# Blockwise causal attention and RWKV channel mix in one kernel: the opening of batch 0 is cut finer and every queue gets a new order

## The chip, the cores and the metric

The kernel runs on one core of one Trainium2 chip, as a single launch. The metric is device time in microseconds (us) of one execution, the median of the runs shown. Inputs are float32 arrays in device memory, the output is a float32 array of 8 x 576 x 512 there; products run in 16-bit types and accumulate in float32.

## The reference

Attention over 8 batches, 8 heads, 576 positions and 64 columns per head, with a mask by blocks of 64 positions; then a channel mix with a token shift over the joined heads. Cut to what matters:

```python
scores = np.matmul(q, k.transpose(0, 1, 3, 2)) / np.sqrt(64)
mask = (pos[:, None] // 64) >= (pos[None, :] // 64)
attn = softmax(np.where(mask, scores, -1e9))          # + 1e-9 in the denominator
x = (attn @ v)                                        # then (B, S, H * D): 8 x 576 x 512
x_prev = x shifted by one position, zero in front
xk = mu_k * x + (1 - mu_k) * x_prev
xr = mu_r * x + (1 - mu_r) * x_prev
kk = np.maximum(xk @ w_k, 0.0)                        # 512 -> 1024
out = sigmoid(xr @ w_r) * ((kk * kk) @ w_v)           # 1024 -> 512
```

## The kernel before

**Attention, batch by batch.** For each batch q and k come in as four tiles of 128 x 1152 float32 (two groups g of four heads, n = 0 for q and 1 for k). Each tile goes through the same steps: a load (tile `t_ld`, queue SP, L272), a cast to bfloat16 (`t_nl`, L251 on ACT or L255 on DVE and POOL), nine transposing products on PE into one PSUM tile (`t_s`, L367; the task is called `turn b g n`), and a copy out of PSUM into `t_qkt` (task `ev b g n`, L251 or L255). In batches 5 to 7 a transposing DMA (L353) does the last two steps instead. v comes as two tiles that are cast to `t_vo`.

Scores are computed transposed (keys on the partitions), in twelve tasks `sc b part i`: `part` 0 or 1 picks which head of a pair, i = 0 to 5 which key blocks (L426). Each is followed by one exponential on ACT (`ex b part i`, L435) into a float16 tile `t_e`. No maximum is taken off first. Then come the column sums of the exponentials, 60 small products with a one-hot matrix `pick` (task `av b 0 S`, L477), and the products with v (`av b 0 A` and `av b 0 B`, L486). DVE transposes the sums (`t1`, L514), takes reciprocals (`rec`, L519), small copies put them in their places (`fix`, L251 or L255), two transposes with broadcast spread them (`t2`, L545), and two multiplications each (`norm`, L555 and L559) write the attention's result to `t_xt`.

**Channel mix, chunk by chunk.** `d` (L581) forms x minus its shifted self, `mul` (L597) forms x + (mu - 1) d into XK and XR, in float16; XK and XR are rings of 1536 rows, so that a chunk of 512 rows crosses batch bounds. There are nine chunks c. For each: `pk c jc` (L644, eight tasks of four products 128x512), a relu (L622 on ACT, L624 on DVE), a square (L630 on ACT, L632 on DVE and POOL) into `t_k`; `pr c jt` (L666, four tasks) with a tanh (L675); `pv c jt` (L694, four tasks of eight products), the gated result on DVE (`o`, L702) and a store (L709). The weights are loaded early, through the same `t_ld` tiles, and cast to WK, WR and WV by tasks `w` (L251, L252, L255, L256).

**What sets the order.** Every step above is a task with a number, its dependences and its buffers. The string ORDER lists the 946 task numbers in the order in which they are issued; each engine and the SP queue carries out its share strictly in that order and waits where an operand or a buffer is missing. The string PLACE picks the engine of every task that more than one engine could do. Buffers are rings: six `t_ld`, four `t_nl`, sixteen `t_e`, three PSUM tiles `t_s` of two banks for turns, scores, sums and products with v, two PSUM tiles `t_mm` of one bank for the channel mix. A load waits in the SP queue until the cast that empties its `t_ld` tile is done, and so holds up what is behind it.

**Unread products.** A word such as `9+14` in ORDER puts 14 extra products 128x512 of the identity with itself ahead of task 9 (L264, function `unread`); they write to a free `t_mm` tile, and nobody reads them. They depend on nothing that comes from device memory, so they run while PE would wait. There are 49 of them, all before the channel mix starts: 14 ahead of the first turn, 9 ahead of the second, 26 ahead of later turns and scores of batches 0 to 2.

In batch 0 every score waits for all four copies `ev 0 g n`, each of 1152 columns:

```python
        deps = [evac[b, g, n] for g in range(2) for n in range(2)]
```

The sums of a batch are one task that waits for all twelve exponentials (`fnS`, L492; `sums`, L460).

## Time and profile before

| | |
|---|---|
| median of 3 runs | 258.75 us (258.72 to 259.55) |
| the profiled execution | 259.53 us; its span is 257.7 us |
| PE busy | 246.6 us, 96% of the span |
| DVE, ACT, POOL busy | 192.4, 181.5, 89.7 us |
| the 49 unread products | 15.7 us of PE's busy time |
| read from and written to device memory | 33.56 and 9.44 MB |

The profile is of one execution; its times are counted from the start of the span. PE is TensorE's matmuls, PEld its weight loads, DVE is VectorE, ACT ScalarE, POOL GpSimd, SP the queue that issues all DMA transfers. A row of the time line gives the start, the duration, the engine, the line, the operation, output and input, the count of merged instructions, and in brackets the engine's idle time just before with what ended it. Idle time of an engine costs only where another waits for it.

### The profile page before, as it was taken

How to read it: one execution, taken by the hardware profiler on the slowest of the kernel's cores; microseconds unless marked ns; L12 is line 12 of the kernel's file. 1: busy time of each engine (PE TensorE's matmuls, PEld its weight loads, DVE VectorE, ACT ScalarE, POOL GpSimd, SP SyncE). 2: the span in 40 equal slices, each digit the busy share in tenths (PEclk: the TensorE clock that was granted, in tenths of full speed). 3: DMA queues.
4: the chain of work that ended last, by engine and by line, in shares of the span. 5: the costliest groups of instructions: out<-in, count | busy, mean ns of one | idle time of the engine just before them, and what ended most of it. 6: DMA issues, size and time to landing. Idle time of an engine off the chain costs nothing.

```text
span 257.7 us, 6524 instructions
## 1 busy us (share of the span) xinstructions
PE 246.6 (96%) x2718; PEld 123.0 (48%) x2718; DVE 192.4 (75%) x274; ACT 181.5 (70%) x251; POOL 89.7 (35%) x74
## 2 busy tenths in 40 slices
PE   7989789999999999999999999999999999999994
PEld 2546454544555445554454454445444544444452
DVE  1814799899779989878799896985997597763412
ACT  1299698987889698676889888687689480550630
POOL 1024384680038313470273103130712543260220
PEclk9999999999999999999999999999999999999999
DMA  7999979979699399996990899999907300303014
GB/s 256 399 265 260 347 237 241 323 217 282 196 274 235 86 188 200 267 198 129 264 149 4 196 174 263 239 154 217 227 6 186 112 4 0 122 0 122 4 61 184
DMA packets 93150, 46.96 MB, mean 182 GB/s; under 512 B 80696, under 2 KB 80960, under 8 KB 93120
## 3 DMA queue, kind: packets, MB, share of 16 engines
q1 hardware_dynamic: 93120, 46.54, 75.4%
q8 instruction: 21, 0.34, 0.6%
q14 instruction: 9, 0.07, 0.1%
HBM read 33.56 MB, written 9.44 MB: 167 GB/s over the span
## 4 chain that ended last, share of the span: by engine, by line
PE 80%; DVE 8%; ACT 6%; POOL 2%; issue 2%; DVEq 0%; POOLq 0%; ACTq 0%
PE t_mm L644 24%; PE t_mm L694 23%; PE t_mm L666 10%; PE t_s L426 8%; PE t_s L486 6%; ACT t_e L435 5%; PE t_s L477 4%; PE t_s L367 3%; PE t_mm L264 3%; DVE t_xt L559 2%; POOL t_k L632 1%; DVE t_rt L545 1%; POOL t_d L581 1%; DVE WV L256 1%; ACT t_qkt L251 1%
## 5 line engine op out<-in xcount | busy, mean ns | idle before, releaser
L435 ACT ACTIVATE t_e<-t_s 128x1024 f16<-128x1024 f32 (+1 forms) x96 | 88.2, 979 | 16.8 <-PE t_s L426 15.0
L644 PE MATMUL t_mm<-XK,WK 128*128 128x512 f16 x288 | 68.5, 379 | 0.3
L694 PE MATMUL t_mm<-WV,t_k 128*128 128x512 f16 (+1 forms) x296 | 66.1, 374 | 0.9 <-DVE WV L256 0.5
L632 POOL TENSOR_TENSOR t_k<-t_kr 128x512 f16<-128x512 f32 x31 | 36.4, 1184 | 59.7 <-ACT t_kr L622 42.6
L622 ACT ACTIVATE t_kr<-t_mm 128x512 f32<-128x512 f32 x55 | 32.6, 598 | 27.8 <-PE t_mm L644 27.5
L694 PEld LDWEIGHTS <-t_k 128*128 128x128 f16 x296 | 27.6, 98 | 34.5 <-issue 3.0
L644 PEld LDWEIGHTS <-WK 128*128 128x128 f16 x288 | 26.5, 97 | 32.9 <-issue 4.9
L702 DVE SCALAR_TENSOR_TENSOR t_o<-t_t,t_mm 128x512 f32<-128x512 f32 (+1 forms) x37 | 24.7, 671 | 22.3 <-PE t_mm L694 13.2
L426 PE MATMUL t_s<-t_qkt 64*64 64x512 bf16 (+7 forms) x640 | 31.0, 290 | 4.1 <-ACT t_qkt L251 2.0
L666 PE MATMUL t_mm<-WR,XR 128*128 128x512 f16 x144 | 34.8, 379 | 0.0
L255 POOL CAST t_vo<-t_ld 128x1152 f16<-128x1152 f32 x12 | 14.3, 1189 | 48.6 <-DVE XR L597 16.1
L597 DVE SCALAR_TENSOR_TENSOR XK<-t_d,MU,t_xt 128x576 f16<-128x576 f32 (+2 forms) x40 | 29.4, 758 | 0.8 <-POOL t_d L581 0.7
L597 DVE SCALAR_TENSOR_TENSOR XR<-t_d,MU,t_xt 128x576 f16<-128x576 f32 (+2 forms) x40 | 28.1, 727 | 0.1
L255 POOL CAST t_nl<-t_ld 128x1152 bf16<-128x1152 f32 x12 | 14.8, 1244 | 32.3 <-DMA t_ld<-in_k_dram 15.7
L675 ACT ACTIVATE t_t<-t_mm 128x512 f32<-128x512 f32 x36 | 21.1, 595 | 6.6 <-PE t_mm L666 6.5
L426 PEld LDWEIGHTS <-t_qkt 64*64 64x64 bf16 x640 | 15.0, 105 | 21.9 <-issue 18.8
L545 DVE STREAM_TRANSPOSE t_rt<-t_rc 128x1152 f32<-128x1152 f32 x16 | 22.0, 1377 | 1.5 <-ACT t_rc L251 1.1
L486 PE MATMUL t_s<-t_e,t_vo 64*64 64x64 f16 (+7 forms) x640 | 22.8, 284 | 0.1
L581 POOL TENSOR_TENSOR t_d<-t_xt 128x1152 f32<-128x1152 f32 x8 | 17.4, 2172 | 10.5 <-DVE t_xt L559 6.8
L666 PEld LDWEIGHTS <-XR 128*128 128x128 f16 x144 | 13.3, 97 | 16.1 <-issue 1.3
L486 PEld LDWEIGHTS <-t_vo 64*64 64x64 f16 x640 | 15.9, 107 | 8.4 <-issue 1.9
L251 ACT COPY t_qkt<-t_s 128x1152 bf16<-128x1152 bf16 x12 | 13.2, 1121 | 9.1 <-PE t_s L367 9.1
(40 smaller groups left out, 205.4 us busy)
## 6 DMA issues: line engine op xcount, KB each, us to landing
t_ld<-in_v_dram SPq DMA_DIRECT2D x32, 288.0 KB, 5.9
out_dram<-t_o SPq DMA_DIRECT2D x35, 256.0 KB, 2.6
t_ld<-in_k_dram SPq DMA_DIRECT2D x10, 576.0 KB, 6.5
t_ld<-in_q_dram SPq DMA_DIRECT2D x10, 576.0 KB, 5.4
t_ld<-in_q_dram SPq DMA_DIRECT2D x12, 288.0 KB, 5.1
t_ld<-in_k_dram SPq DMA_DIRECT2D x12, 288.0 KB, 5.7
t_ld<-in_moe_w_k_dram SPq DMA_DIRECT2D x4, 512.0 KB, 6.7
t_ld<-in_moe_w_v_dram SPq DMA_DIRECT2D x4, 512.0 KB, 5.7
```

The source lines that it names most:

```text
L255: return e.tensor_copy(dst, src)
L426: nc.tensor.matmul(PS[g * D:g * D + D, x, col:col + n], qkt[rows, ka:ka + D], qkt[rows, qa:qa + n], start=True, stop=True)
L435: nc.scalar.activation(new(ebuf[key])[:, :, 0:width], new(m)[:, :, 0:width], AF.Exp, scale=ISQ)
L486: nc.tensor.matmul(dst(slice(y * D, (y + 1) * D), u, x, q0, n), new(vo_buf[b])[u * D:u * D + D, 2 * x + y, t], new(ebuf[key])[u * D:u * D ...
L545: nc.vector.transpose(new(rt[x])[:, 0:2 * W].rearrange("p (n r) -> p n r", r=QC), new(rc)[:, x].rearrange("p u n -> p (u n)").unsqueeze(2) ...
L597: return nc.vector.scalar_tensor_tensor((XK, XR)[kr][:, cc, g:g + w], new(d)[:, u * n + at - lo:u * n + at - lo + w], MU1[:, kr, cc:cc + 1 ...
L622: nc.scalar.activation(new(kr), new(m), AF.Relu)
L632: return e.tensor_tensor(dst(), KR, KR, ALU.mult)
L644: nc.tensor.matmul(ps, WK[:, cc, jc * P:(jc + 1) * P], XK[:, cc, at:at + CH], start=(cc == 0), stop=(cc == CCn - 1))
L666: nc.tensor.matmul(ps, XR[:, cc, g % R:g % R + P], WR[:, cc], start=(cc == 0), stop=(cc == CCn - 1))
L694: nc.tensor.matmul(ps[:, 0:w], k2[:, jc, jt * P:(jt + 1) * P], WV[:, jc, cols], start=(jc == 0), stop=(jc == JCn - 1))
L702: nc.vector.scalar_tensor_tensor(new(o)[:, 0:w], new(tb)[:, cols], 1.0, new(m)[:, 0:w], ALU.add, ALU.mult)
```

## The change

Four things are edited, and the rest of the program is as it was.

1. The copies out of the turns of batch 0 are cut in two along the transposed columns: half y (0 or 1) holds the keys and queries of `part` y. Each copy `ev 0 g n` of 1152 columns becomes `ev 0 g n 0` and `ev 0 g n 1` of 576, each with an engine of its own. A score of part y waits only for the four halves y.
2. The sums of batch 0 are two tasks on the same PSUM tile: `av 0 0 P` with the 40 products that need only the exponentials i = 0 to 3, and `av 0 0 S` with the remaining 20, which goes on in the same accumulation.
3. ORDER has new numbers throughout (951 tasks), with 36 unread products instead of 49: 9 ahead of the first turn instead of 14, then none, 3 and 3 ahead of the other turns of batch 0 where 9, none and 1 stood.
4. PLACE is new. All four copies of batch 1's turns are on DVE (two were on ACT); batch 0's first cast and all four of batch 1's are on POOL.

The core of the diff (ORDER and PLACE cut to a line):

```diff
-7 8 9+14 10 11 12 13+9 15 16 17 18 3 4 5+1 6 96 14 49+4 50 61 57 58 62
+13 14 15+9 0 1 18 19 20 21 22 3 4 8 9 5+3 6 7 101 102 93 94 17 10+3 11
...
+        parts = 2 if b == 0 else 1
+        for y in range(parts):
+            def ev(eng, me, y=y):
+                pst = new(m)[:, :, :].rearrange("p a b -> p (a b)").bitcast(BF)
+                w, h = 2 * S // parts, P // parts
+                convert(eng, new(qkt_buf[b])[
+                    :, at + y * w:at + y * w + w].rearrange(
+                        "q (p j) -> q p j", j=JT),
+                    pst[:, 0:2 * S].rearrange("q (j p) -> q p j", p=P)[
+                        :, y * h:y * h + h])
...
-        deps = [evac[b, g, n] for g in range(2) for n in range(2)]
+        deps = [evac[b, g, n, part if b == 0 else 0]
+                for g in range(2) for n in range(2)]
...
+        FIRST = 4 if b == 0 else 0
...
+                if (key[2] < FIRST) != early:
+                    continue
...
+            opens = 4 if early or not FIRST else 0
+            ends = len(runs) if early else len(runs) - 4
             for n_, (c, a, z, j, t, src, _) in enumerate(runs):
                 nc.tensor.matmul(
                     PA[c * QC:(c + 1) * QC, a:z], pick[:, j], src,
-                    start=n_ < 4, stop=n_ >= len(runs) - 4)
+                    start=n_ < opens, stop=n_ >= ends)
...
+            exps = exps + [add(
+                f"av {b} {part} P", "PE", lambda eng, me: fnS(eng, me, True),
+                [ready[key] for key in some],
+                [m["S"]] + [ebuf[key] for key in some])]
```

**Place one: DVE, from its first cast on.** `t_nl` are casts of loaded tiles (`t_ld`), `t_qkt` copies out of PSUM, `t_tt` the transposed sums. Before:

```order
L255 CAST t_nl_67<-t_ld_58 128x2x9x64
L255 COPY t_qkt_74<-t_s_152 128x1152
L255 CAST t_nl_68<-t_ld_59 128x2x9x64
L255 CAST t_nl_69<-t_ld_60 128x2x9x64
L255 CAST t_nl_70<-t_ld_61 128x2x9x64
L255 COPY t_qkt_74<-t_s_153 128x1152
L255 CAST t_nl_67<-t_ld_63 128x2x9x64
```

After:

```order
L255 CAST t_nl_68<-t_ld_59 128x2x9x64
L255 CAST t_nl_69<-t_ld_60 128x2x9x64
L255 CAST t_nl_70<-t_ld_61 128x2x9x64
L255 COPY t_qkt_74<-t_s_154 128x576
L255 COPY t_qkt_74<-t_s_152 128x576
L255 COPY t_qkt_74<-t_s_153 128x576
```

The first tile's cast has gone to POOL, and no copy stands between the casts of batch 0 any more. Behind these rows DVE now has one more half copy, the four copies of batch 1 (`t_qkt_75`), one cast of batch 2 and then the sums; before, it had two of batch 1's copies and two more casts ahead of the sums.

**Place two: ACT, from the last exponentials of batch 0 on.** `t_e` are exponentials, `t_qkt` copies out of the turns, `t_rc` the small copies of the reciprocals. Before:

```order
L435 ACTIVATE t_e_94<-t_s_154 128x2x320
L435 ACTIVATE t_e_95<-t_s_153 128x2x320
L251 COPY t_qkt_75<-t_s_154 128x1152
L251 COPY t_qkt_75<-t_s_152 128x1152
L251 COPY t_rc_112<-t_rc_112 32x36 x4
L251 COPY t_qkt_74<-t_s_154 128x1152
L435 ACTIVATE t_e_96<-t_s_154 128x1024
```

After:

```order
L441 ACTIVATE t_e_94<-t_s_152 128x1024
L441 ACTIVATE t_e_95<-t_s_153 128x1024
L441 ACTIVATE t_e_96<-t_s_154 128x1024
L251 COPY t_rc_112<-t_rc_112 32x36 x2
L441 ACTIVATE t_e_97<-t_s_153 128x1024
L441 ACTIVATE t_e_98<-t_s_153 128x1024
```

The three copies of turns between batch 0's exponentials and batch 1's are gone from there; `t_e_96`, batch 1's first exponential, stands ahead of the reciprocals' copies.

**Place three: DVE, from the last weight cast on.** WV is the cast of w_v, `t_d` the difference, XK and XR the mixes, `t_o` the gated results of chunk 0. Before:

```order
L256 TENSOR_SCALAR WV<-t_ld_58 128x1024
L597 SCALAR_TENSOR_TENSOR XK<-t_d_121,MU_176,t_xt_104 128x576
L581 TENSOR_TENSOR t_d_122<-t_xt_104 128x1152
L597 SCALAR_TENSOR_TENSOR XR<-t_d_122,MU_176,t_xt_104 128x576
L597 SCALAR_TENSOR_TENSOR XK<-t_d_122,MU_176,t_xt_104 128x576
L702 SCALAR_TENSOR_TENSOR t_o_145<-t_t_138,t_mm_159 128x512
L702 SCALAR_TENSOR_TENSOR t_o_146<-t_t_141,t_mm_158 128x512
```

After:

```order
L256 TENSOR_SCALAR WV<-t_ld_59 128x1024
L601 TENSOR_TENSOR t_d_121<-t_xt_104 128x1152
L617 SCALAR_TENSOR_TENSOR XR<-t_d_121,MU_176,t_xt_104 128x576
L617 SCALAR_TENSOR_TENSOR XK<-t_d_121,MU_176,t_xt_104 128x576
L722 SCALAR_TENSOR_TENSOR t_o_145<-t_t_138,t_mm_159 128x512
L617 SCALAR_TENSOR_TENSOR XR<-t_d_122,MU_176,t_xt_104 128x576
L617 SCALAR_TENSOR_TENSOR XK<-t_d_122,MU_176,t_xt_104 128x576
```

Three XR mixes now stand ahead of or between the four XK mixes of batch 1, where one stood; DVE has one `d`, seven mixes and three gated results to do from here to the last XK mix, five mixes, one `d` and three gated results before.

28 lines of the change are left out of this document (13 added, 15 removed), and 102 rows, old and new, of the table ORDER.

## The prediction, on record before the run

> **What bounds the kernel now.** I read the page's busy times first, then the table by stretches, then the time line of the first 60 us.
>
> ```profile
> PE 246.6 (96%) x2718; PEld 123.0 (48%) x2718; DVE 192.4 (75%) x274; ACT 181.5 (70%) x251; POOL 89.7 (35%) x74
> DMA  7999979979699399996990899999907300303014
> ...
> 0.00:40.00 40.00, 33.25 (x435) 19.02 (x436) 22.96 (x33) 27.30 (x33) 13.67 (x15) 1.00 0.99 291
> 40.00:60.00 20.00, 19.36 (x265) 9.59 (x264) 19.04 (x27) 18.35 (x27) 12.34 (x10) 1.00 0.90 261
> 60.00:240.00 180.00, 179.54 (x1949) 87.20 (x1946) 144.43 (x206) 130.01 (x185) 60.35 (x46) 1.00 0.75 158
> 240.00:258.00 18.00, 14.47 (x75) 7.15 (x73) 6.00 (x10) 5.80 (x10) 3.33 (x3) 1.00 0.24 89
> ...
> L264 PE MATMUL t_mm<-identb 128*128 128x512 bf16 x49 | 15.7, 441 | 1.4 <-POOL identb masks.py:199 1.4
> ```
>
> In the second to fifth rows the columns are the stretch, PE, PEld, DVE, ACT, POOL busy, clock, DMA share, GB/s. From 60 to 240 us PE is busy 179.54 of 180: there is nothing to win, only something to lose. The waste is in the first 40 us: 6.75 us idle and 15.7 us of unread products, which PE fills its waits with. All other PE work is the same after the change, so the time moves with one quantity: how soon the head lets PE run without waits. I take the start of the first `pv` as the mark.
>
> ```profile
> 1.36 5.59 PE L264 MATMUL t_mm<-identb 128*128 128x512 bf16 x14 [1.36 <-POOL identb masks.py:199]
> 4.28 0.76 DVE L255 CAST t_nl<-t_ld 128x1152 bf16<-128x1152 f32 x1 [2.39 <-DMA t_ld<-in_k_dram]
> 6.79 0.67 PE L367 MATMUL t_s<-identb,t_nl 128*128 128x128 bf16 x9
> 7.29 2.11 PE L264 MATMUL t_mm<-identb 128*128 128x512 bf16 x9
> 7.49 1.36 DVE L255 COPY t_qkt<-t_s 128x1152 bf16<-128x1152 bf16 x1 [2.45 <-PE t_s L367]
> 8.77 2.09 DVE L255 CAST t_nl<-t_ld 128x1152 bf16<-128x1152 f32 x3
> 10.96 2.14 ACT L251 COPY t_qkt<-t_s 128x1152 bf16<-128x1152 bf16 x2 [8.94 <-PE t_s L367]
> 13.61 10.46 ACT L435 ACTIVATE t_e<-t_s 128x1024 f16<-128x1024 f32 x12 [0.51 <-PE t_s L426]
> 24.22 2.14 ACT L251 COPY t_qkt<-t_s 128x1152 bf16<-128x1152 bf16 x2 [0.15 <-PE t_s L367]
> 26.44 0.48 DVE L514 STREAM_TRANSPOSE t_tt<-t_s 128x288 f32<-128x288 f32 x1 [3.42 <-ACT t_qkt L251]
> ...
> 27.59 0.91 ACT L251 COPY t_rc<-t_rc 32x36 f32<-32x36 f32 x4 [1.23 <-DVE MU L296]
> ...
> 30.16 1.02 ACT L435 ACTIVATE t_e<-t_s 128x1024 f16<-128x1024 f32 x1 [0.51 <-PE t_s L426]
> ...
> 31.69 1.02 ACT L435 ACTIVATE t_e<-t_s 128x1024 f16<-128x1024 f32 x1 [0.51 <-PE t_s L486]
> ...
> 39.71 2.18 PE L644 MATMUL t_mm<-XK,WK 128*128 128x512 f16 x8
> ...
> 56.67 2.39 DVE L256 TENSOR_SCALAR WV<-t_ld 128x1024 f16<-128x1024 f32 x2
> ...
> 59.20 3.61 PE L694 MATMUL t_mm<-WV,t_k 128*128 128x512 f16 x16 [0.50 <-DVE WV L256]
> ```
>
> The reader sees a chain: the first tile is cast at 5.04, but its turn starts only at 6.79, because fourteen products stand ahead; DVE then holds three casts behind a copy; ACT starts its exponentials at 13.61 and has none left over; the sums reach DVE at 26.44, when ACT's copies are done; from there DVE works almost without a gap until the last WV cast ends at 59.06, and `pv` starts 0.14 later.
>
> **The change, step by step.**
>
> *First turn.* Fourteen products take 5.59 before the turn, 0.40 each, the first ones slower; at 0.43 nine end at 1.36 + 9 x 0.43 = 5.2. The first tile's cast is now POOL's:
>
> ```profile
> 13.79 1.14 POOL L255 CAST t_nl<-t_ld 128x1152 bf16<-128x1152 f32 x1 [12.49 <-DMA t_ld<-in_k_dram]
> ...
> t_ld<-in_k_dram SPq DMA_DIRECT2D x1, 576.0 KB, 3.5
> ...
> t_ld<-in_k_dram SPq DMA_DIRECT2D x1, 576.0 KB, 8.6
> ```
>
> (The last two rows are the first load, issued at 0.73, and the seventh, issued at 5.07: size and time to landing.) The first lands at 4.2, POOL ends at 5.4, the turn starts at 5.5 instead of 6.79. The two small loads of mu are now second in SP's queue; the tiles behind them are spaced by the transfers, not by their issue: (13.7 - 4.2)/6 = 1.58 us from tile to tile. I cost them at nothing, at most 0.8 (two issues).
>
> *Fourth tile and first exponential.* The fourth tile lands at 4.2 + 3 x 1.58 = 9.0; DVE has no copy ahead of it now (before, its cast ended at 10.86, behind the copy at 7.49 and two casts). Cast to 9.8, turn to 10.5. A half copy costs between half a whole one and a whole one, 0.56 to 1.12 on ACT and 0.68 to 1.36 on DVE; a 36-column copy takes 0.91/4 = 0.23, mostly fixed, so I take 0.66 and 0.75. ACT's last half for part 1 ends at 11.2, DVE's second half at 11.3; the score takes 0.4, the first exponential starts near 11.9, 1.7 sooner. But the second score task in PE's order is of part 0 and waits for DVE's fourth half (12.8); the second exponential, a score behind it on PE, starts at about 13.6, so ACT loses 0.7: 1.0 is left.
>
> *Batch 0's exponentials.* Twelve take 10.46: at best 11.9 + 0.7 + 10.46 = 23.1. Batch 1's four copies, now all DVE's, and its turns lie between them on PE. The turn of tile 1 1 1 stands ahead of the last three scores; it is the ninth load, 4.2 + 8 x 1.58 = 16.8, cast on POOL at 18.0. With a PSUM tile `t_s` passed on to each whole copy of 1.36 us, I walk the queues to 23.9 (before: 24.07). Ends: 23.1 and 24.6.
>
> *Sums.* 40 of 60 products run while the last exponential does; 20 remain:
>
> ```profile
> 46.65 1.43 PE L477 MATMUL t_s<-t_e,pick 128*32 128x288 f16 x60
> ```
>
> 1.43/3 = 0.5. `P` stands behind batch 1's first score on PE, which needs batch 1's last copy (22.2 by the same walk), so that it holds nothing up. t1 starts at 24.7 (ends 24.3 and 25.4) instead of 26.44: **-1.7 us**. Before, ACT's two copies at 24.22 stood between; they are now DVE's, hidden under exponentials.
>
> *DVE from t1 to the last WV cast.* Before: 59.06 - 26.44 = 32.6, nearly all busy. After, the list lacks one cast, one whole copy, one relu, one v cast and four small copies, and has one WK cast, two squares and one WV cast more:
>
> ```profile
> 44.97 1.27 DVE L624 TENSOR_SCALAR t_kr<-t_mm 128x512 f32<-128x512 f32 x2
> 46.17 0.74 DVE L255 CAST t_vo<-t_ld 128x1152 f16<-128x1152 f32 x1
> 49.37 0.78 DVE L255 COPY t_rc<-t_rc 32x36 f32<-32x36 f32 x4
> ...
> L632 DVE TENSOR_TENSOR t_k<-t_kr 128x512 f16<-128x512 f32 x17 | 12.7, 776 | 4.2 <-ACT t_kr L622 4.1
> ```
>
> Less: 0.76 + 1.36 + 0.64 + 0.74 + 0.78 = 4.3. More: 0.75 (the other casts) + 2 x 0.78 + 1.2 = 3.5. **-0.8 us.** New waits: the reciprocals' copies stand behind batch 1's exponentials on ACT (up to 1.0 each, two places). The second sums wait for batch 1's last exponential. Where sums and products with v hold two PSUM tiles, batch 1's exponentials share the third and come 31.69 - 30.16 = 1.53 apart; after, five do so from 26.3 to 33.5, three more follow at 0.9 apiece (36.2), then three whole copies at 1.13 (39.6), three exponentials and a relu (43): sums near 43.2 instead of 46.65, just ahead of the second t1 in DVE's list. Together **+0.5**, ends 0 and 2.
>
> *PE.* One score task fewer lies ahead of the first `pv`: **+0.2**. PE itself does not bind: from the first `pk` (39.71 before; about 37.5 after, 2.2 sooner with the XK mixes) it has at most 17.2 us of work to the first `pv` (the 19.5 of before less some waits). If DVE were faster than I think, PE's bound would be near 54.7, a gain of 4.5: the low end.
>
> Sum: -1.7 - 0.8 + 0.5 + 0.2 = **-1.8 us**. After the mark I count nothing: PE waits 0.46 us in 180 now, and the tail's order is of the same kind. Unread products saved are no gain of their own (13 x 0.22 to 0.43): they lie in waits. Against the profiled 259.53 (span 257.7 and 1.8 around it) that is 257.7; the median lies 0.8 lower than that execution, so I predict 258.75 - 1.8 = **256.9 us**.
>
> **Rivals.**
>
> *The clock gate opens late (no change).* The first fourteen products go at 0.43, the nine from 7.29 on at 2.11/9 = 0.23: the gate opened in between, after about 5 us without a pause. Nine products are only 3.9 us, with pauses behind. Then three products cost 1.3 instead of 0.65 and a turn 1.0 instead of 0.5 ahead of tiles three and four: turns end near 10.2 and 12.4 instead of 10.5 for the fourth, the first exponential starts at 13.8, and the sums gain only about 0.4: 258.2. Against it: the turn follows within 0.3 us. The Trainium skill ("TensorE: Matmul & The Clock Gate", Part 1 and Part 4) says that about 3.4 us of activity in a free-running window opens the gate, and that transposes do not count as activity in the same way. By that rule nine products fill a window only if its phase is lucky, which speaks against this change; the trace agrees as to the size of the step, and cannot show the shorter run. Chance 0.16.
>
> *DVE is late for chunk 1 (slower).* After the first `pv`, PE has four `pv`, five scores and a turn, 4 x 1.83 + 5 x 0.22 + 0.5 = 8.9 us, until `pk 1` needs the last XK mix of batch 1.
>
> ```profile
> 58.98 0.81 DVE L597 SCALAR_TENSOR_TENSOR XK<-t_d,MU,t_xt 128x576 f16<-128x576 f32 x1
> 59.70 1.35 DVE L581 TENSOR_TENSOR t_d<-t_xt 128x1152 f32<-128x1152 f32 x1
> ...
> 34.22 2.66 DVE L597 SCALAR_TENSOR_TENSOR XK<-t_d,MU,t_xt 128x576 f16<-128x576 f32 x2
> ...
> L702 DVE SCALAR_TENSOR_TENSOR t_o<-t_t,t_mm 128x512 f32<-128x512 f32 (+1 forms) x37 | 24.7, 671 | 22.3 <-PE t_mm L694 13.2
> ...
> 87.71 0.50 PE t_s L367 x9
> 88.21 0.56 PE t_s L426 x16
> 88.77 1.83 PE t_mm L694 x8
> ```
>
> DVE has from the mark on one `d`, seven mixes and three results: 1.35 + 7 x 0.81 + 3 x 0.67 = 9.0, no slack. Mixes beside POOL's work took 2.66/2 = 1.33: then 12.7, and PE idles 3.8. The time is lost for good, since PE is full behind it: 256.9 + 3.8 less what is won back = 260.2. It decides for "slower" from 1.8 + 0.8 = 2.6 us of idle on. For it: two mixes fewer stood there before. Against it: the mixes of this very stretch took 0.81 (58.98). Chance 0.13.
>
> *The head doesn't move.* Transfers are at full share for 40 us; if the ninth load or v lands later than the rows say, the halves only wait elsewhere: 258.75. Chance 0.03.
>
> **How the numbers follow.** About 0.3%, 0.8 us, is what a measurement can tell: bounds 258.0 and 259.5. My forecast (gains of 0.8 to 4.5 us, with the larger ones) has 0.68, all faster; the gate and the unmoved head 0.19, same; chunk 1 0.13, slower. The range runs from 258.75 - 4.5 = 254.3 to 259.3, which takes in the gate's case and a chunk 1 that idles 2.4 us.
>
> **What would show it.** First turn near 5.5, first exponential near 11.9, t1 near 24.7, a batch 1 exponential before the reciprocals' copies, last WV cast ending near 57.2 with `pv` behind it, and PE full from 60 on. Wrong would be: spaces of 0.43 between products after 8 us (the gate), idle of PE ahead of the first `pk 1` beyond 1 us (chunk 1), or t1 after 26.

## The result and the profile after

The changed kernel takes 260.71 us (median of 15 runs, 259.97 to 261.75) beside 259.29 for the kernel before on the same chip (15 runs, 258.57 to 260.06): a ratio of 1.0063, 95% interval 1.0051 to 1.0075. It is slower by 0.6%. The forecast was 256.9 us, with a range of 254.3 to 259.3 and a chance of 0.13 for slower. The profiled execution took 260.70 us, its span is 258.9.

The page's busy times and the table by stretches of the kernel after (stretch, PE, PEld, DVE, ACT, POOL, clock, DMA share, GB/s):

```profile
PE 243.6 (94%) x2705; PEld 122.1 (47%) x2705; DVE 198.2 (77%) x279; ACT 175.1 (68%) x248; POOL 91.6 (35%) x76
...
0.00:40.00 40.00, 29.78 (x407) 16.98 (x407) 22.30 (x33) 24.16 (x31) 16.20 (x18) 0.96 0.97 279
40.00:60.00 20.00, 18.83 (x266) 9.75 (x266) 18.31 (x23) 18.18 (x30) 12.78 (x10) 1.00 0.88 277
60.00:240.00 180.00, 179.24 (x1961) 87.79 (x1954) 151.23 (x215) 126.19 (x179) 59.52 (x46) 1.00 0.73 159
```

From 60 us on almost nothing has changed: PE is busy 179.24 of 180 us, 0.3 less than before. The loss lies in the first 40 us, where PE's idle time went from 6.75 to 10.22 us and the clock column reads 0.96 instead of 1.00. The time line of the kernel after, on PE, POOL, DVE and ACT, with the marks that the prediction named:

```profile
1.36 4.02 PE L264 MATMUL t_mm<-identb 128*128 128x512 bf16 x9 [1.36 <-POOL identb masks.py:199]
4.61 1.14 POOL L255 CAST t_nl<-t_ld 128x1152 bf16<-128x1152 f32 x1 [3.31 <-DMA t_ld<-in_q_dram]
5.81 0.68 PE L367 MATMUL t_s<-identb,t_nl 128*128 128x128 bf16 x9 [0.43 <-POOL t_nl L255]
8.80 0.76 DVE L255 CAST t_nl<-t_ld 128x1152 bf16<-128x1152 f32 x1 [6.91 <-DMA t_ld<-in_k_dram]
9.62 1.14 PE L367 MATMUL t_s<-identb,t_nl 128*128 128x128 bf16 x9 [2.98 <-DVE t_nl L255]
10.55 1.49 PE L264 MATMUL t_mm<-identb 128*128 128x512 bf16 x3
10.80 1.18 ACT L251 COPY t_qkt<-t_s 128x576 bf16<-128x576 bf16 x2 [8.79 <-PE t_s L367]
11.74 0.76 DVE L255 CAST t_nl<-t_ld 128x1152 bf16<-128x1152 f32 x1 [0.73 <-DMA t_ld<-in_k_dram]
12.83 2.75 DVE L255 COPY t_qkt<-t_s 128x576 bf16<-128x576 bf16 x4 [0.33 <-PE t_s L367]
13.62 0.64 ACT L251 COPY t_qkt<-t_s 128x576 bf16<-128x576 bf16 x1 [1.64 <-DVE t_qkt L255]
14.95 0.64 ACT L251 COPY t_qkt<-t_s 128x576 bf16<-128x576 bf16 x1 [0.69 <-DVE t_qkt L255]
16.10 1.02 ACT L441 ACTIVATE t_e<-t_s 128x1024 f16<-128x1024 f32 x1 [0.52 <-PE t_s L431]
28.33 0.48 DVE L534 STREAM_TRANSPOSE t_tt<-t_s 128x288 f32<-128x288 f32 x1 [1.63 <-PE t_s L490]
40.55 0.68 PE L367 MATMUL t_s<-identb,t_nl 128*128 128x128 bf16 x9 [1.46 <-POOL t_nl L255]
41.89 1.02 PE L664 MATMUL t_mm<-XK,WK 128*128 128x512 f16 x4 [0.31 <-DVE XK L617]
59.03 0.68 DVE L256 TENSOR_SCALAR WV<-t_ld 128x1024 f16<-128x1024 f32 x1
60.30 2.98 PE L714 MATMUL t_mm<-WV,t_k 128*128 128x512 f16 x13
```

The first turn is early (5.81; forecast 5.5, before 6.79). Then PE stands still for 2.98 us, because the second tile is cast only at 8.80; the second turn takes 1.14 where the first took 0.68, and three products take 1.49, so PE runs at half clock there. ACT's third and fourth half copies are released by DVE's half copies, not by the turn. The first exponential comes at 16.10 (before 13.61), t1 at 28.33 (26.44), the first `pk` at 41.89 (39.71). Between the first `pk` and the first `pv` the kernel wins something back: 18.4 us instead of 19.5, and `pv` follows PE's own work, no longer the last WV cast. So the mark is 60.30 instead of 59.20, 1.1 us late; the span is 1.2 us longer.

### The profile page after: what moved, and what is told of

It reads as the page before. It is cut to its first block, busy times and chain, and to the rows that moved or that the text cites. A ratio compares the mean times of both kernels' runs of the same rounds, so it can differ in the third digit from the quotient of the medians.

```text
span 258.9 us, 6490 instructions
## 1 busy us (share of the span) xinstructions
PE 243.6 (94%) x2705; PEld 122.1 (47%) x2705; DVE 198.2 (77%) x279; ACT 175.1 (68%) x248; POOL 91.6 (35%) x76
## 4 chain that ended last, share of the span: by engine, by line
PE 81%; DVE 10%; ACT 3%; DMA 3%; issue 2%; POOL 1%; SPq 0%; DVEq 0%; POOLq 0%
PE t_mm L714 25%; PE t_mm L664 22%; PE t_mm L686 12%; PE t_s L431 8%; PE t_s L499 7%; PE t_s L490 4%; PE t_s L367 3%; DMA t_ld<-in_k_dram 3%; ACT t_e L441 2%; DVE XK L617 2%; DVE t_qkt L255 2%; DVE t_rt L565 1%; DVE t_d L601 1%; DVE XR L617 1%; POOL WK L255 1%
## 5 line engine op out<-in xcount | busy, mean ns | idle before, releaser
L652 POOL TENSOR_TENSOR t_k<-t_kr 128x512 f16<-128x512 f32 x30 | 33.9, 1137 | 83.3 <-ACT t_kr L642 48.3
L642 ACT ACTIVATE t_kr<-t_mm 128x512 f32<-128x512 f32 x57 | 33.6, 597 | 28.3 <-PE t_mm L664 27.8
L431 PE MATMUL t_s<-t_qkt 64*64 64x64 bf16 (+7 forms) x640 | 30.8, 290 | 3.9 <-ACT t_e L441 1.9
L255 POOL CAST t_nl<-t_ld 128x1152 bf16<-128x1152 f32 x15 | 18.2, 1220 | 37.8 <-DMA t_ld<-in_q_dram 11.3
L695 ACT ACTIVATE t_t<-t_mm 128x512 f32<-128x512 f32 x36 | 20.9, 598 | 12.8 <-PE t_mm L686 12.6
L255 POOL CAST t_vo<-t_ld 128x1152 f16<-128x1152 f32 x12 | 15.6, 1308 | 20.0 <-DVE t_nl L255 6.2
L652 DVE TENSOR_TENSOR t_k<-t_kr 128x512 f16<-128x512 f32 x20 | 16.0, 813 | 7.7 <-ACT t_kr L642 7.7
L601 POOL TENSOR_TENSOR t_d<-t_xt 128x1152 f32<-128x1152 f32 x8 | 17.2, 2155 | 10.7 <-DVE t_nl L255 4.6
```

Of the source, the lines that this page charges most:

```text
L255: return e.tensor_copy(dst, src)
L431: nc.tensor.matmul(PS[g * D:g * D + D, x, col:col + n], qkt[rows, ka:ka + D], qkt[rows, qa:qa + n], start=True, stop=True)
L642: nc.scalar.activation(new(kr), new(m), AF.Relu)
L652: return e.tensor_tensor(dst(), KR, KR, ALU.mult)
```

## The experiments

Three suspects stood in these rows: the late second tile (mu's loads ahead of it in SP's queue), the half copies that wait for each other, and the stretch at half clock. Fourteen kernels take them apart. They are told in three groups. Each ratio compares with the kernel before on the same chip (259.2 to 259.4 us); a difference in us between kernels of different groups goes across chips. In the diffs from the changed kernel 0 is `mus` (mu's two loads), 1 the small product on PE that turns them, 13 and 18 are the first and second tile's loads, 15 and 20 their turns.

### Mu's loads

**Mu's loads seventh in the queue** (task 1 goes later with them; nothing else):

```diff
-13 14 15+9 0 1 18 19 20 21 22 3 4 8 9 5+3 6 7 101 102 93 94 17 10+3 11
+13 14 15+9 18 19 20 21 22 3 4 8 9 5+3 6 7 101 102 93 0 94 17 10+3 11 12
...
```

> The changed kernel with the two small loads of mu moved from second place in SP's queue to seventh, behind six tile loads, and their small transposing product on PE moved from behind the first turn to behind the sixth turn. Theory S (the small loads hold up the tiles behind them): the second tile lands near 6.1 instead of 8.8, the first exponential starts near 12 to 13.5 instead of 16.10, t1 near 25.5 instead of 28.33, the first pv near 58 instead of 60.30; the time is 1.5 to 2.6 us below the changed kernel's, about 258.5, ratio to before 0.994 to 0.999. Theory C (the small loads do nothing, the late tiles are the price of the other order of loads or chance): second tile near 8.8 again, ratio to before 1.005 to 1.007 as for the change.

Measured: 258.75 us, ratio 0.9979 (0.9963 to 0.9995), 2.0 us under the changed kernel. Its time line on DVE and ACT:

```profile
6.74 0.76 DVE L255 CAST t_nl<-t_ld 128x1152 bf16<-128x1152 f32 x1 [4.85 <-DMA t_ld<-in_k_dram]
...
9.75 0.76 DVE L255 CAST t_nl<-t_ld 128x1152 bf16<-128x1152 f32 x1 [0.73 <-DMA t_ld<-in_k_dram]
...
14.25 1.02 ACT L441 ACTIVATE t_e<-t_s 128x1024 f16<-128x1024 f32 x1 [0.52 <-PE t_s L431]
```

The second and the fourth tile come 2.0 us sooner, and t1 1.85 us sooner (26.48). This one edit turns the loss into a small gain. Two things in this trace are as instructive. The first tile is now cast later, at 5.34 instead of 4.61, and the first turn starts at 6.54: the early first turn of the changed kernel came in part from mu's place. And from 7.45 to 10.86 us the clock is at half here too, behind a wait of 1.76 us for the first tile's cast, so moving the loads does not take the third suspect away.

**Mu's loads second in the queue of the kernel before:**

```diff
-7 8 9+14 10 11 12 13+9 15 16 17 18 3 4 5+1 6 96 14 49+4 50 61 57 58 62
+7 0 8 9+14 10 11 12 13+9 15 16 17 18 3 4 5+1 6 96 14 49+4 50 61 57 58 62
...
```

> The kernel before with one edit: the two small loads of mu go from seventh to second place in SP's queue. Theory S: the second tile lands 2 to 3 us later than 6.0, the first exponential starts 2 us or more behind 13.61, and the time grows by 1.5 to 2.7 us, ratio to before 1.006 to 1.010. Theory C: second tile at 6.0 to 6.3, ratio 1.000 within 0.001.

Measured: 260.12 us, ratio 1.0024 (1.0010 to 1.0038). The order of before pays 0.6 to 0.8 us for it, less than the 1.5 that were expected at least: its first exponential moves by 0.38 only (13.99 instead of 13.61), where its tiles waited for DVE's copy and casts already; t1 moves by 1.1 (27.54). How the transfers go in each, by stretches of 1 us of the changed kernel, of the one with mu late, and of before with mu early (the last two columns are DMA share and GB/s):

```profile
4.00:5.00 1.00, 1.00 (x4) 0.20 (x2) 0.00 (x0) 0.00 (x0) 0.39 (x1) 1.00 0.64 177
5.00:6.00 1.00, 0.57 (x5) 0.19 (x5) 0.00 (x0) 0.00 (x0) 0.76 (x1) 1.00 0.89 283
6.00:7.00 1.00, 0.65 (x10) 0.45 (x7) 0.00 (x0) 0.00 (x0) 0.00 (x0) 1.00 0.97 320
```

```profile
4.00:5.00 1.00, 0.78 (x4) 0.15 (x2) 0.00 (x0) 0.00 (x0) 0.00 (x0) 1.00 1.04 410
5.00:6.00 1.00, 0.00 (x0) 0.00 (x0) 0.00 (x0) 0.00 (x0) 0.66 (x1) 1.00 1.05 346
```

```profile
4.00:5.00 1.00, 1.00 (x4) 0.35 (x3) 0.52 (x1) 0.00 (x0) 0.00 (x0) 1.00 0.83 237
```

With mu's loads between the first and the second tile the transfers slump at 4 us to 177 GB/s (237 in the order of before) where 410 flow without them. In the changed kernel they stay low for four more microseconds (283, 320, 325, 334), in the order of before for none (396 at 5 us). Mu's eight packets of 512 bytes run from 3.57 to 3.87 us in the changed kernel's trace and from 3.61 to 3.75 in this one, just ahead of the slump. Task 1 stayed where it was in this kernel, so the loads alone do it.

**Mu's loads ahead of the first tile:**

```diff
-13 14 15+9 0 1 18 19 20 21 22 3 4 8 9 5+3 6 7 101 102 93 94 17 10+3 11
+0 13 14 15+9 1 18 19 20 21 22 3 4 8 9 5+3 6 7 101 102 93 94 17 10+3 11
...
```

> The changed kernel with mu's two small loads ahead of the first tile instead of behind it (small product on PE behind the first turn, 9 products, as in the changed kernel). Theory S in the form that small transfers between two tiles break the stream: the slow stretch of the transfers from 4 us on is gone or comes before the first tile, the second tile lands near 7 (0.9 for the issue of the small ones), and the time is 1 to 2 us below the changed kernel's, ratio to before 0.998 to 1.002. If small transfers cost the same wherever they stand near the front: second tile at 8.5 or later, ratio 1.004 to 1.007.

Measured: 259.29 us, ratio 1.0003 (0.9990 to 1.0016). The second tile is cast at 7.44, the fourth at 10.45: 0.7 us later than with mu late, which is what the two issues take in SP's queue. There is no slump (373 GB/s at 4 us).

**Rows of q instead of mu, in the same place** (beside 15 more unread products in PE's waits, as in the kernel called "after, waits filled" below, with which it is to be compared):

```diff
-                              src.rearrange("(c p) -> c p", p=P))
+                              q[0, 4 + n, 0:2 * CCn].rearrange(
+                                  "(c y) d -> c (y d)", y=2))
```

> As the one before, but the two small loads that stand second and third in SP's queue read 18 rows of 512 bytes from the first tile's own part of q instead of mu's two tensors (so the mixes use wrong factors; the work is the same). Theory one, the small packets or the two more transfers in the queue slow the tiles behind them: the second tile lands near 8.8 us as before, and the time is within 0.3 us of the one before. Theory two, it is the first touch of two more tensors: no slump after 4 us, the second tile lands at 6.7 to 7.4, first exponential 1.4 to 2 us sooner, and the time is 0.8 to 1.5 us lower.

(The text on record says 18 rows of 512 bytes; it is eight, four for each load.) Measured: 260.13 us (258.76 to 261.12), against 260.17 for the kernel with mu itself. The transfers fall to 224 GB/s at 4 us and the second tile is cast at 8.33, with mu itself at 8.58. So it is not the first touch of two other tensors; two small loads in this place do it when they read q as well.

**Mu's loads on ACT's queue, at its start** (also beside the filled waits):

```diff
-            nc.sync.dma_start(MUR[CCn * n:CCn * n + CCn, :],
+            nc.scalar.dma_start(MUR[CCn * n:CCn * n + CCn, :],
...
-    mu_rows = add("mus", "SP", mus)
+    mu_rows = add("mus", "ACT", mus)
```

> As the changed kernel with PE's waits filled (260.2), but mu's two loads are issued from ACT's queue at its start, not from SP's. If it is the place in SP's queue that delays the tiles behind them: the second tile lands at 6.4 to 7.0 us, the time falls to 258.3 to 258.8. If it is the transfers themselves, wherever they are issued: the second tile still lands after 8 us, and the time stays at 259.8 to 260.3.

Measured: 258.98 us (median of 12, 258.69 to 261.79), ratio 1.0007 (0.9983 to 1.0031). By the medians that is 1.2 us under the 260.17 with them in SP's queue, by the ratios 0.9, and the two intervals overlap; what is clear of noise here is the tile, not the time. The profiled run is the slowest of the twelve, 261.79; why is told with the clock. The first rows of SP's and of ACT's queue, and DVE's cast of the second tile:

```profile
0.73 0.46 SPq L272 DMA_DIRECT2D t_ld<-in_q_dram  x1
1.25 0.45 SPq L272 DMA_DIRECT2D t_ld<-in_k_dram  x1
```

```profile
0.73 0.56 ACTq L284 DMA_DIRECT2D MUR<-in_moe_mu_k_dram  x1
1.32 0.26 ACTq L284 DMA_DIRECT2D MUR<-in_moe_mu_r_dram  x1
```

```profile
6.71 0.76 DVE L255 CAST t_nl<-t_ld 128x1152 bf16<-128x1152 f32 x1 [4.82 <-DMA t_ld<-in_k_dram]
```

The second tile is issued at 1.25 and cast at 6.71, 5.5 us later, as in the kernel with mu late (1.24 to 6.74). In the changed kernel it is issued at 1.98 and cast at 8.80, 6.8 us later. So of the 2.06 us that mu's place costs the second tile (8.80 against 6.74) 0.74 are the two issues in SP's queue, and 1.3 a slower way from issue to landing. From ACT's queue the transfers do the second tile no harm. The queue and the moment are not quite separated by that run, since its two loads go out beside the first tile, not behind it. But four of their eight packets run at 3.72 to 3.94 us, the moment of the changed kernel's, and the rate at 4 us is 408 GB/s. So one trace speaks for the place in SP's queue, not for the moment of the transfers. The Trainium skill ("DMA: Bandwidth & Descriptors", Issuing engines are not separate DMA queues) says that another issuing engine saves only the time of the issue; by that rule 0.74 us would be won, and the runs show 2.0 on the tile.

### The half copies

**Mu late, and 14 products ahead of the first turn as before.** This is the base of the next three:

```diff
-13 14 15+9 18 19 20 21 22 3 4 8 9 5+3 6 7 101 102 93 0 94 17 10+3 11 12
+13 14 15+14 18 19 20 21 22 3 4 8 9 5+3 6 7 101 102 93 0 94 17 10+3 11 12
...
```

> As the first kernel (mu's loads seventh), and with 14 unread products ahead of the first turn instead of 9. Theory G: nine products with pauses behind them leave the gate half closed until about 10 us, so 14 are better by 0.3 to 1.0 us than the first kernel. Rival: the fourth tile sets the first exponential and PE has time to catch up from the first turn's 1.3 us delay: equal within 0.3 us.

Measured: 259.02 us, ratio 0.9982 (0.9966 to 0.9998), no different from nine products (258.75).

**Both halves of a turn on one engine, the half for part 1 first** (ACT has the tiles 0 1 1 and 0 0 1, DVE the other two):

```diff
-13 14 15+14 18 19 20 21 22 3 4 8 9 5+3 6 7 101 102 93 0 94 17 10+3 11 12
+13 14 15+14 18 19 20 22 21 3 4 17 8 9 5+3 101 102 93 0 94 10+3 7 6 12 11
...
-    "DDADDAPDDDAAPPPPPDPPDADDAADPPDPDPDPDPPAADPPAPAPDDAAPDDPDAAPADDADP"
+    "DDDDAAPDDDAAPPPPPDPPDADDAADPPDPDPDPDPPAADPPAPAPDDAAPDDPDAAPADDADP"
...
```

> As the run with mu's loads seventh and 14 products ahead of the first turn, with one more edit: both halves of a turn are copied by one engine (two turns each on ACT and DVE), the part 1 half first. Theory H (two engines that read one PSUM tile are made to wait for each other, so that the split halves run one after the other and the split gains nothing): no copy waits for the other engine any more, the first exponential starts near 12.4 to 12.8 instead of 13.90, t1 near 25.0 instead of 26.13, and the time falls by 0.5 to 1.2 us, ratio to before 0.994 to 0.997. Rival L (batch 1's loads and copies, between batch 0's scores on PE, set the sums, so a sooner first exponential is only waited away): t1 within 0.4 of 26.13, ratio 0.997 to 0.999.

**Whole copies again** (three on ACT, that of tile 0 1 0 on DVE and earlier in the order; the rest in the order of the base, renumbered):

```diff
-        parts = 2 if b == 0 else 1
+        parts = 1
...
-        deps = [evac[b, g, n, part if b == 0 else 0]
+        deps = [evac[b, g, n, 0]
```

> As the run with mu's loads seventh and 14 products ahead of the first turn, with batch 0's copies out of the turns whole again (three on ACT, one on DVE), everything else in the same order. Theory H: the split gained nothing, so the first exponential starts near 13.1 to 13.6, at or before 13.90, and the time is equal or up to 0.5 us lower, ratio to before 0.996 to 0.999. Rival (the split works as meant): the first exponential starts later than 13.90, and the time grows by 0.3 to 1 us, ratio 1.000 to 1.002.

Measured: 258.11 us, ratio 0.9948 (0.9927 to 0.9969), paired; 257.46 us, ratio 0.9942 (0.9920 to 0.9965), whole. ACT's rows of the base, of the paired halves and of the whole copies:

```profile
8.48 1.18 ACT L251 COPY t_qkt<-t_s 128x576 bf16<-128x576 bf16 x2 [6.46 <-PE t_s L367]
11.41 0.64 ACT L251 COPY t_qkt<-t_s 128x576 bf16<-128x576 bf16 x1 [1.76 <-DVE t_qkt L255]
12.74 0.64 ACT L251 COPY t_qkt<-t_s 128x576 bf16<-128x576 bf16 x1 [0.69 <-DVE t_qkt L255]
13.90 1.02 ACT L441 ACTIVATE t_e<-t_s 128x1024 f16<-128x1024 f32 x1 [0.52 <-PE t_s L431]
```

```profile
8.28 1.18 ACT L251 COPY t_qkt<-t_s 128x576 bf16<-128x576 bf16 x2 [6.27 <-PE t_s L367]
11.29 1.18 ACT L251 COPY t_qkt<-t_s 128x576 bf16<-128x576 bf16 x2 [1.83 <-PE t_s L367]
12.45 1.02 ACT L441 ACTIVATE t_e<-t_s 128x1024 f16<-128x1024 f32 x1
```

```profile
8.30 2.30 ACT L251 COPY t_qkt<-t_s 128x1152 bf16<-128x1152 bf16 x2 [6.29 <-PE t_s L367]
10.96 1.12 ACT L251 COPY t_qkt<-t_s 128x1152 bf16<-128x1152 bf16 x1 [0.37 <-PE t_s L367]
12.60 5.85 ACT L441 ACTIVATE t_e<-t_s 128x1024 f16<-128x1024 f32 x6 [0.52 <-PE t_s L431]
```

In the base ACT waits for DVE twice, since the two halves of one turn stand in one PSUM tile and the second reader is held until the first is done. Each half is quick (0.59 to 0.64 us), but two engines on one tile take turns. Paired, ACT waits only for PE, and the first exponential comes 1.45 us sooner; whole copies do as well, 1.3 us sooner. So the cut into halves buys nothing here beside whole copies, and as the change placed it, it costs about 1 us (1.15 among the runs with the clock up throughout, and 1.05 with the waits filled, both below). The Trainium skill ("PSUM — Partial Sum Buffer", PSUM bank collisions raise a hardware error) says that no two engines may access one bank in the same partitions at once, reads included, and that dependences keep them apart; the waits in this trace agree. It would have been the rule that speaks against this change. That the chip itself needs the wait was not tried.

**One sum task** in the base (the 60 products together, after the last exponential):

```diff
-        FIRST = 4 if b == 0 else 0
+        FIRST = 0
```

> As the run with mu's loads seventh and 14 products ahead of the first turn, with batch 0's sums in one task again (all 60 products behind the last exponential). If the early part was worth what the prediction put on it: t1 0.8 to 0.9 us later than 26.13, and the time up by 0.3 to 0.9 us, ratio to before 0.999 to 1.002. If t1 is waited away later: ratio 0.998, as without the edit.

Measured: 259.56 us, ratio 1.0005 (0.9991 to 1.0018), 0.5 us over the base. From the first exponential to t1 it takes 12.63 us (13.67 to 26.30) against the base's 12.23 (13.90 to 26.13). So the early sums are worth about 0.4 us up to t1, under half of the 0.8 to 0.9 that were expected. How much of it reaches the end is blurred by the clock, below: among runs of equal granted clock the difference is 0.2 us (clock up throughout) and 0.6 (one fall to half).

### The granted clock

Each run comes with its mean granted clock. The kernel before has 0.998 or more in every run beside the experiments. The changed kernel has 0.992 or 0.993 in 11 of 15 runs (median 260.70) and 0.986 or 0.987 in the other four (median 261.67); none is above 0.993. In the record of the clock, each time that it falls to half within the work it does so for 3.413 us: 3.413/2 is 0.66% of the span, so these are runs with one and with two such stretches. In the changed kernel's profile it lies from 9.02 to 12.43 us, and begins in the 2.98 us of idle PE:

```profile
8.00:9.00 1.00, 0.00 (x0) 0.00 (x0) 0.20 (x1) 0.00 (x0) 0.00 (x0) 1.00 0.97 334
9.00:10.00 1.00, 0.38 (x4) 0.38 (x5) 0.56 (x1) 0.00 (x0) 0.00 (x0) 0.51 1.01 385
10.00:11.00 1.00, 1.00 (x10) 0.72 (x8) 0.74 (x1) 0.20 (x1) 0.00 (x0) 0.50 1.06 415
```

The same division by granted clock for the kernels that had both kinds of runs (medians in us, number of runs in brackets):

| kernel | 0.998 to 1.000 | 0.991 to 0.993 | 0.985 to 0.987 |
|---|---|---|---|
| mu late | 258.46 (6) | 258.95 (2) | 259.76 (4) |
| mu late, 14 products | 258.46 (4) | 259.16 (7) | 260.13 (1) |
| halves paired | 257.31 (2) | 258.23 (4) | |
| whole copies | 257.31 (4) | 258.48 (2) | |
| one sum | 258.67 (3) | 259.77 (9) | |
| mu ahead of the first tile | 259.21 (6) | 259.51 (6) | |
| seven products in the wait | 259.53 (5) | 261.19 (4) | 261.57 (3) |
| after, waits filled | 260.09 (3) | 260.84 (4) | |
| rows of q | 260.12 (10) | 260.61 (2) | |
| mu on ACT's queue | 258.92 (10) | 260.70 (2) | |
| mu late, 14, waits filled | 258.29 (7) | 259.24 (2) | |

Runs with one stretch at half clock are 0.3 to 1.8 us slower than runs with none. The two do not differ by the clock alone, though: the ten runs of 0.998 or more with mu on ACT's queue lie between 258.69 and 260.99, and one of the five such runs with seven products in the wait took 261.54. The profiles show three places for the stretch. One is the head. One is behind PE's wait for the half copies ahead of the first score (1.26 to 1.55 us, in the profiles of mu first, mu on ACT's queue, and mu late with 14 products and filled waits: from 16.05, 17.49 and 14.94). One is the wait for POOL's cast of batch 2's third tile (1.46 us ahead of 40.55 in the changed kernel): with one sum task the clock is at half from 40.22 to 43.64, and four products take 1.52 instead of 1.02:

```profile
38.51 0.68 PE L367 MATMUL t_s<-identb,t_nl 128*128 128x128 bf16 x9 [1.47 <-POOL t_nl L255]
...
39.85 1.52 PE L664 MATMUL t_mm<-XK,WK 128*128 128x512 f16 x4 [0.31 <-DVE XK L617]
```

The order of before has no such wait between its turns of batch 2 (0.25 us at most). A wait of this size doesn't always do it: the profile of mu late with 14 products has the same 1.46 us ahead of 38.35 and no fall, and the kernel before waits 1.35 us ahead of 29.70 in its profile, where the clock stays up. The change left out 13 unread products; whether they kept the clock up is what the next kernels try.

**Seven products in the wait for the second tile:**

```diff
-13 14 15+9 0 1 18 19 20 21 22 3 4 8 9 5+3 6 7 101 102 93 94 17 10+3 11
+13 14 15+9 0 1 18 19 20+7 21 22 3 4 8 9 5+3 6 7 101 102 93 94 17 10+3 11
...
```

> The changed kernel with seven unread products ahead of its second turn, where PE idles from 6.64 to 9.62. Theory G (a good part of the loss is the clock gate that closes in this idle time): PE's clock stays full from 6 us on, turns two and three take 0.67 instead of 1.14 and 0.96 and three products 0.8 instead of 1.49, the first exponential starts 0.7 to 1.3 sooner than 16.10, and the time falls by 0.5 to 1.2 us, ratio to before 1.001 to 1.004. If the gate costs little beside the late tiles: ratio 1.005 to 1.007. If seven products run at half clock (0.43 each) they end at 9.6, with no gain and no loss.

Measured: 261.19 us, ratio 1.0045 (1.0023 to 1.0067): as slow as without them, in the median. The first exponential is 0.56 us sooner (15.54), but in the profiled run the half-clock stretch moved to 41.20 to 44.61. The expected gain of 0.5 to 1.2 us came only where the clock stayed up: of the twelve runs five have no such stretch (median 259.53), four have one (261.19), three two (261.57).

**The same, and eight products in the wait at 37 to 40 us** ("after, waits filled"):

```diff
...
-159 83 86 123 124 131 132 172+1 173 164 160 165 161 119 84 33 34 166 167
+159 83 86 123 124 131+2 132 172+1 173 164 160+6 165 161 119 84 33 34 166
...
```

> The changed kernel with mu's loads where the change put them, with 7 unread products in PE's 3-us wait for the second tile and 8 in the wait at 37 to 40 us; nothing else. Theory of the gate: the clock stays open (0.998 or more in nearly all runs) and the median is 259.4 to 259.7, which is 1.0 to 1.3 under the changed kernel's 260.7; what is left above e4's 258.5 with an open gate is the late tiles. Rival (the gate costs nothing, since PE waits there anyway): 260.4 to 260.8.

Measured: 260.17 us (7 runs), ratio 1.0041 (1.0024 to 1.0058): only half of the gain that was expected, with an interval that overlaps the changed kernel's (1.0051 to 1.0075), and four of the seven runs have a granted clock of 0.991 to 0.993. The profiled one, with 1.000, shows why the head is not mended:

```profile
5.83 1.14 PE L367 MATMUL t_s<-identb,t_nl 128*128 128x128 bf16 x9 [0.46 <-POOL t_nl L255]
...
7.11 3.17 PE L264 MATMUL t_mm<-identb 128*128 128x512 bf16 x7
```

Here the clock goes up only at 10.69 us, as the lengths tell (a turn 1.14, products 0.45 each; the clock column reads 1.00 until the first entry of the record). The seven products then last 3.17 us and end behind the second tile's cast at 9.34. Filling a wait that shouldn't be there is a poor remedy.

The mean granted clock says nothing of such a late start, which lies ahead of the first entry of the record. In the profiles that entry comes between 4.04 and 7.22 us, but for two: this one, and mu on ACT's queue with 10.66 (seven products in 3.10 us, first exponential at 15.82 although the second tile was there at 6.71). Both have nine products ahead of the first turn. Of the seven profiled kernels with nine, two start late, of the nine with fourteen none; that is too few to call it shown.

**The same eight products in the kernel with mu late and 14 products ahead:**

```diff
...
-159 83 86 123 124 131 132 172+1 173 164 160 165 161 119 84 33 34 166 167
+159 83 86 123 124 131+2 132 172+1 173 164 160+6 165 161 119 84 33 34 166
...
```

> The changed kernel with mu's loads seventh in the queue, 14 products ahead of the first turn, and 8 unread products more in the wait at 35 to 38 us; half copies as the change has them. Theory of the gate: nearly all runs at 0.998 or more, median 258.3 to 258.6 (e4's open runs: 258.46). Then the differences between this, the whole copies and the changed kernel, all with an open gate, are the prices of the half copies (1.0 to 1.2 us) and of mu's place (0.9 to 1.2 us). Rival: as without the fills, 259.0, with closed gates in over half of the runs.

Measured: 258.33 us, ratio 0.9965 (0.9951 to 0.9980); seven of nine runs at 0.998 or more. Without the eight it was 259.02, with four of twelve. The profiled run is one of the other two. Its clock is at half from 14.94 to 18.35, behind a wait that the eight products don't fill:

```profile
13.32 0.41 PE L431 MATMUL t_s<-t_qkt 64*64 64x512 bf16 x4 [1.55 <-ACT t_qkt L251]
```

**And in the kernel with whole copies:**

```diff
...
-119 120 127 128 168+1 169 160 156 161 157 115 80 29 30 162 163 27 28 548
+119 120 127+2 128 168+1 169 160 156+6 161 157 115 80 29 30 162 163 27 28
...
```

> The kernel with mu's loads late, 14 products ahead and whole copies in batch 0, and 8 unread products more where PE waits for POOL's cast at about 35 us (6 ahead of turn 2 0 0, 2 ahead of the last score before it). Theory of the gate: its runs without a closed gate were at 257.3 us, those with one closure at 258.5, so with the wait filled nearly all runs have a granted clock of 0.998 or more and the median is 257.2 to 257.5, with no run above 258. Rival (the two groups of runs come from something else than the clock): the runs spread as before, 256.9 to 258.8, median 257.5 to 257.8, and the clock of some is still 0.993.

Measured: 257.28 us, all six runs between 257.17 and 257.58 and at a clock of 0.999 or more; ratio 0.9921 (0.9907 to 0.9935). This is the fastest kernel here. Beside the half copies with the waits filled (258.33) it is 1.05 us faster, and the intervals are apart: that is the price of the half copies. What the eight products add is less sure: 257.28 against 257.46, six of six runs with the clock up against four of six. PE's rows:

```profile
35.40 1.46 PE L264 MATMUL t_mm<-identb 128*128 128x512 bf16 x6
37.03 0.68 PE L367 MATMUL t_s<-identb,t_nl 128*128 128x128 bf16 x9 [0.17 <-POOL t_nl L255]
...
38.37 1.02 PE L664 MATMUL t_mm<-XK,WK 128*128 128x512 f16 x4 [0.32 <-DVE XK L617]
...
56.78 3.63 PE L714 MATMUL t_mm<-WV,t_k 128*128 128x512 f16 x16
```

The turn starts no sooner for the six products, since POOL's cast sets it; only the clock is kept. The mark is at 56.78, 2.4 us sooner than before, and PE has no wait of DVE's in front of it.

**Mu's loads second again in that kernel:**

```diff
-11 12 13+14 15 16 17 18 3 4 7 8 14 5+3 6 97 98 89 0 90 9+3 10 55+2 56
+11 0 12 13+14 15 16 17 18 3 4 7 8 14 5+3 6 97 98 89 90 9+3 10 55+2 56
...
```

> As the kernel with whole copies, late mu and filled waits (257.3), but with mu's loads second and third in SP's queue again; 14 products stand ahead of the first turn. If mu's place has a price of its own: second tile after 8 us, first exponential at 14.4 to 14.9 instead of 12.9, time 258.8 to 259.3. If the price is only that which the order of before showed: 257.8 to 258.1.

Measured: 258.98 us (12 runs, all at 0.998 or more), ratio 0.9988 (0.9974 to 1.0002). With the clock up throughout and no half copies, mu's place costs 1.7 us: the second tile is cast at 7.87 instead of 6.52, the first exponential starts at 14.18 instead of 12.86, the mark is at 58.40 instead of 56.78:

```profile
7.87 0.76 DVE L255 CAST t_nl<-t_ld 128x1152 bf16<-128x1152 f32 x1 [5.98 <-DMA t_ld<-in_k_dram]
...
14.18 5.86 ACT L441 ACTIVATE t_e<-t_s 128x1024 f16<-128x1024 f32 x6 [0.52 <-PE t_s L431]
```

## Why the prediction was wrong

- **The step that failed first: mu's loads, costed "at nothing, at most 0.8 (two issues)".** The issues alone are 0.74, and the transfers behind them are slower by 1.3 more. The fourth tile was to land at 9.0 and is cast at 11.74. Moving the two loads back is worth 2.0 us in the changed kernel and 1.7 in the one with whole copies and filled waits. The spacing of 1.58 us from tile to tile, read from the kernel before, held behind the second tile (1.46 and 1.48); it didn't hold ahead of it, where the casts of the first two tiles start 4.19 us apart, and 1.40 with mu late.
- **The second: the half copies, with ACT's last for part 1 at 11.2 and DVE's at 11.3, side by side.** From the fourth tile's cast to the first exponential I had 2.9 us; it took 4.36. In the base kernel it took 3.95, paired 2.69 (9.76 to 12.45), whole 3.17 (9.43 to 12.60). The durations of a half were right (0.66 and 0.75 taken; 0.64 and 0.69 measured); that two engines read one tile in turn was missing. Together the two steps make the first exponential late by 4.2 us: 2.7 for the tile, and 1.45 behind it. Of these about 1.05 are the copies (3.95 in the base, at full clock, against 2.9); the rest goes with the half clock, at which the last turn starts 1.54 us after its tile's cast does, 0.82 in the base.
- **The rival of the gate came about, in another form.** The first turn did follow within 0.43 us and ran at full clock, and the clock fell to half later, in the wait of 2.98 us that the late tile made. In four of the fifteen runs it fell a second time; no profile of this kernel shows where, those of three others have a fall at 39 to 41 us. Filling the waits moved the median by 0.5 us (260.71 to 260.17), which is not clear of the noise; the sign that the prediction named, spaces of 0.43 between products after 8 us, is there at 10.55 (three products in 1.49). In its own form, a first turn at half clock behind nine products, the rival shows in two other kernels' profiles (clock up at 10.66 and 10.69), not in this one's; the changed kernel's other fourteen runs can't tell. The rule of a free-running window of about 3.4 us that the prediction took from the Trainium skill ("TensorE: Matmul & The Clock Gate", Part 1) fits every stretch seen here: half clock for 3.413 us each, and times at full clock of 10, 72 and 73 such lengths (34.133, 245.760 and 249.173 us in the record). I weighed it only for the first nine products, not for every wait of the head.
- **Right: from the first exponential to t1.** 12.8 us were forecast (11.9 to 24.7), 12.23 came (16.10 to 28.33). The two sum tasks bring about 0.4 us of that, where the prediction took two thirds of 1.43, that is 0.95, off the way.
- **Right in sign, too small: from t1 to the mark.** -0.8 for DVE's list, +0.5 and +0.2 made -0.1; measured 31.97 us against 32.76, -0.8. DVE's last WV cast ended 59.71 - 28.33 = 31.4 us after t1, 1.2 sooner than before. But "PE itself does not bind" was wrong: from the first `pk` to the mark PE takes 18.41 us, 18.11 of them busy, in the changed kernel and in the one with whole copies and filled waits alike (38.37 to 56.78), not 17.2. The kernel before could have told: of its 19.5 us there PE is busy for 18.85.
- **Right: after the mark nothing is lost.** 198.5 us of span follow it before, 198.6 after; PE's one new wait is 0.76 us long. The rival of a DVE that is late for chunk 1 did not happen.

The sum, against the span: t1 +1.9 instead of -1.7, the way to the mark -0.8 instead of -0.1, behind it +0.1: +1.2. With mu's loads late, whole copies and 13 more products (five ahead of the first turn, eight in the later wait) it is 257.28 against 259.23, -1.95. That this is close to the -1.8 of the forecast is in part luck: t1 is at 24.81, as forecast (24.7), but from there to the mark it wins another 0.8 where I had 0.1, and it has no half copies and as many unread products as the kernel before. Between it and the changed kernel lie 3.4 us, for two details of the order and the waits that they opened. (The 258.75 that the forecast starts from is the median of three runs; fifteen give 259.29, which moves the forecast to 257.5 and saves nothing.)

Open is why the way from issue to landing grows when two small loads stand between the first two tiles: by 1.3 us in the changed kernel, by 1.1 in the same with waits filled (1.98 to 8.58), by 0.4 with whole copies (1.99 to 7.87), by none when they stand ahead of the first tile (1.93 to 7.44) or on the other queue.

## What to carry to other kernels

A transfer of a few kilobytes is not free where it stands: put between the first two tiles of a load stream it delayed all that followed by 1.3 to 2 us, put ahead of the first by 0.7, and with them each step that waits for a tile. Where a copy out of PSUM is cut for two engines, cut by tile, not within a tile, or look in the trace for one engine's copy that is released by the other's. When an order loses unread products, go through every wait of PE over 1 us that is left: the clock may fall to half behind it, in some runs only, so look at the granted clock of all runs, not of the profiled one, and at how long the first products take, which that clock doesn't show.

## What the runs showed of the hardware

- Two loads of 2 KB each between the first and the second tile: transfers at 177 GB/s instead of 410 from 4 to 5 us, and the second tile's way from issue to cast 6.8 us instead of 5.5. From another queue at the same time as the first tile: 5.5 and no slump (408 GB/s at 4 us).
- The granted clock fell to half for 3.413 us at a time; a wait of PE of 1.47 us stands ahead of the fall in one profile (one sum task), and one of 1.46 in another without a fall (mu late, 14 products). Runs of one kernel with one fall were 0.3 to 1.8 us slower in the median than runs with none.
- Half a copy of 1152 columns took 0.59 to 0.64 us on ACT and 0.69 to 0.75 on DVE, little over half of the whole (1.12 and 1.36).
